# Loading the first four chunks of a gated linear attention two tokens to a partition, ahead of a fused MLP

## The chip, the cores and the metric

The kernel runs on one NeuronCore of a Trainium2 chip. The metric is device time in microseconds (us), taken over whole executions; five runs of the kernel before are shown, and one execution was recorded by the hardware profiler. Engines are named as in the profile: PE is TensorE's matmul side and PEld its weight loads, DVE is VectorE, ACT is ScalarE, POOL is GpSimd, SP is SyncE, which here only issues DMAs.

## The reference

Inputs q, k, v and alpha have the shape (4, 8, 768, 48): 4 batches, 8 heads, 768 tokens, 48 values a head, all f32. A recurrence with a decaying state gives the attention output, which then goes through an MLP with the gate h cos(h):

```
state = zeros(B, H, D, D)
for t in range(S):
    state = alpha[:, :, t, :, None] * state + k[:, :, t] (outer) v[:, :, t]
    y[:, :, t] = q[:, :, t] @ state
x = y as (B * S, H * D)            # 3072 tokens x 384
h = x @ w_in                       # 384 x 2048
out = (h * cos(h)) @ w_out         # 2048 x 384
```

## The kernel before

The recurrence is done in chunks of 128 tokens: 6 chunks a batch, 24 in all, and two neighbouring chunks make a pair (g = j // 2). Within a chunk, logarithms of alpha are summed by a matmul with a triangular matrix; exponentials of the sums scale k and q; scaled k and q are transposed; scores k·q are masked to the lower triangle; the output is scores times v plus the state of the chunk before times q; the state is updated and decayed. Heads are handled two at a time, in 64 rows each, of which 48 are used.

All work is written as units, a letter and a number each, and the string ORDER fixes the order in which they are issued. Each engine runs its own units in that order and each DMA queue too. The last loop of the kernel just walks through ORDER. The letters that matter here:

- `a k q v`: load of one chunk of alpha, k, q or v, on the SP queue (L158, L161): 128 partitions (tokens) by 8 heads by 48 values, so 1024 rows of 192 B, 192 KB.
- `w`: a half of w_in (w0, w1) or of w_out (w2, w3), on POOL's DMA queue, cast to bf16 on the way (L167, L171).
- `i`/`l`, `c`/`C`, `d`/`E`: logarithm on ACT (L185), cumulative sums on PE (L191, L193), two exponentials on ACT (L201, L202), for one chunk or for a pair.
- `K`/`B` and `R`/`O`: scaling of k (L206) and of q (L212), on POOL or on DVE. `P`: cast of v to bf16 on POOL (L216). `M`: the chunk's decay on POOL (L220).
- `T`, `t`: transposes on PE (L227) and their copy out of PSUM by DVE (L232). `D`: the same by a DMA transpose on the SP queue (L236).
- `A`, `m`: scores on PE (L243) and their masking on DVE (L248). `S`, `u`, `b`: the state's matmuls (L257), its update on DVE (L262 or L272), its decay on POOL (L262).
- `Y`, `y` or `Q`, `z`: outputs of a chunk or of a pair on PE (L298), copied to the MLP's input xT by DVE (L306, L317).
- `F`/`H`, `f`/`h`, `p`/`g`: first MLP product on PE (L337), cosine on ACT as a shifted sine (L343), gate on DVE (L348). F works on one chunk and half of the 2048 columns, H on a pair and a quarter. F0 and F2 need w0, F1 and F3 need w1. `V`: a quarter of the second product (L358); `e`: its copy by ACT (L362); `o`: store on the SP queue (L366).
- `x12`: twelve matmuls on zeros (L371), which keep PE running while it has nothing else.

ACT loads another function table whenever it passes from logarithms and exponentials to sines or back (L179, L343). PSUM is handed out from two small pools, 3 tiles of two banks (`two`) and 2 of one bank (`one`). An instruction that waits on one engine holds all that stand behind it on that engine, and a DMA that waits holds the rest of its queue. On the SP queue, each DMA from the ninth on also waits for the one eight places before it to have landed.

Of the kernel before, what the change touches and what calls it, by code (L numbers as in the profile page):

```python
# [9 lines left out]
FP = mybir.dt.float32  # L10
# [7 lines left out]
k1 a0 a3 a1 k0 v1 q0 a2 q2 i0 x12 c0 v3 d0 k2 M0 i1 x7 c1 k3 K0 d1 q1 K1 q3 P1 O0 x13 T0 v0 l1 t0  # L18
a5 x2 C1 E1 a4 v2 K2 q5 R2 K3 k5 x15 T2 O1 t2 T1 k4 A0 t1 q4 P0 x1 A1 w0 S1 S0 a6 u0 w1 u1 l2 M1
m0 R3 x8 C2 w2 m1 T3 E2 M2 Y0 w3 t3 A2 y0 P2 Y1 m2 b1 S2 A3 M3 P3 u2 M4 m3 b2 Q1 x6 F0 z1 y1 S3 f0  # L20
F2 p0 f2 x2 F3 p2 F1 f3 H6 p3 f1 H4 p1 h6 u3 V4 h4 g6 b3 V5 V0 g4 V1 v4 H5 a7 V2 h5 v5 R5 V3 g5 V6
a8 e0 K5 V7 a9 H7 K4 e1 q6 R4 T5 h7 V8 t5 k6 V9 g7 T4 v9 P4 V10 t4 v6 V11 l3 S4 e2 A4 q7 u4 A5 P5
C3 m4 b4 o2 V12 E3 m5 V13 k7 S5 Q2 l4 u5 M7 M6 o0 R6 C4 z2 a11 M5 K6 V14 E4 H10 v7 b5 q8 T6 P6 k8
H8 t6 h10 R7 q11 S6 a10 V15 h8 g10 K7 H9 q9 e3 u6 g8 M9 T7 k9 M8 h9 H11 t7 k10 P7 g9 V16 h11 v8 R8
S7 A6 u7 A7 o1 V17 m6 b7 V20 a13 m7 V21 V18 a12 l5 g11 Q3 o3 R9 C5 z3 v10 K8 V19 E5 H12 K9 D8 e4
R11 H14 D9 M10 P8 H13 h12 K10 o4 q10 k11 g12 S8 h13 V22 v11 V23 u8 h14 q12 g13 H15 b8 e5 P10 k12
g14 V28 M11 k13 h15 P9 S10 V29 a15 g15 V30 a14 A8 R10 l6 A9 m8 V31 v12 K11 C6 e7 m9 E6 S9 D10 P11
Q4 u9 b9 D11 V24 z4 R12 V25 u10 v13 H18 K12 v14 b10 H16 D12 h18 H19 q15 g18 h16 o5 P12 S11 g16 h19
H17 M12 v15 u11 o7 V26 g19 h17 V27 a16 P13 V32 g17 e6 M13 A10 q13 A11 m10 S12 V33 o6 l7 V34 a17
m11 C7 k14 Q5 E7 a18 u12 A12 z5 P15 V36 R15 V37 m12 K13 V38 H22 R13 M15 H20 D13 b11 h22 P14 H21  # L30
q19 g22 K14 h20 q17 q14 V35 g20 v16 h21 V39 k15 q21 e8 H23 g21 e9 o9 V40 h23 S13 V41 u13 R14 g23
A13 V44 b13 l8 D14 V45 m13 V46 K15 q20 V47 v17 C8 D15 Q6 E8 P16 q16 V42 z6 a19 e11 V43 M16 R17 k17
H24 o8 q18 P17 k16 M14 S14 a21 h24 H25 u14 b14 e10 g24 S15 h25 o10 H26 R16 k18 g25 V48 h26 K17 H27
u15 g26 D17 b15 V52 h27 V53 a20 K16 v18 A15 A14 a23 m15 V49 D16 l9 V50 m14 V54 v19 C9 g27 Q7 E9
K18 V55 z7 V51 R18 e13 H28 o13 e12 R19 a22 o12 S16 M18 D18 S17 u16 H30 h28 b16 o11 g28 H29 q23 P19
h30 k19 P18 v22 M17 u17 V60 q22 h29 g30 V56 H31 g29 l10 A17 A16 m17 V61 V62 K19 m16 h31 V57 D19
V58 g31 C10 k20 Q8 E10 V59 z8 V63 R20 e14 H32 o14 e15 b17 k21 o15 K20 S18 k23 S19 u18 H34 h32 v21
R21 u19 D20 M19 g32 H33 b19 h34 v20 K21 v23 V68 g34 h33 k22 M20 V64 D21 H35 g33 P21 l11 A18 A19
m18 V69 V70 P20 m19 M21 h35 V65 V66 g35 C11 Q9 E11 P22 V67 z9 P23 K23 V71 e16 H36 o16 e17 M22 R23
o17 S20 R22 D23 H38 u20 h36 b20 H37 g36 h38 K22 M23 S21 D22 g38 h37 V76 H39 u21 g37 b21 V72 h39  # L40
A21 A20 m21 V77 V78 m20 V73 V74 g39 A22 Q10 V75 z10 V79 e18 m22 H40 o18 e19 o19 S23 h40 S22 H42
u22 b22 g40 H41 h42 u23 V80 b23 g42 h41 H43 g41 A23 h43 V84 m23 V81 g43 V82 Q11 V83 z11 V85 e20
H45 o20 V86 h45 H44 g45 H47 h44 H46 g44 h47 V87 g47 h46 V88 e21 V89 g46 o21 V92 V93 V90 V91 V94
e22 V95 o22 e23 o23
# [22 lines left out]
def kernel(  # L67
# [21 lines left out]

    sb = ctx.enter_context(tc.tile_pool(name="sb", bufs=1))  # L90
# [20 lines left out]
    nc.vector.memset(halfpi, math.pi / 2.0)  # L111
    ident_bf = sb.tile([C, C], BF, tag="ident_bf")
# [11 lines left out]
    make_upper_triangular(nc, mask_f, 1.0, diag=True)  # L124
    m2 = sb.tile([C, 2], FP, tag="m2")
# [6 lines left out]
    a_t = ring("a_sb", [C, 2, H, D], FP, 4)  # L132
    k_t = ring("k_sb", [C, H, D], FP, 6)
    q_t = ring("q_sb", [C, H, D], FP, 6)
    v_t = ring("v_sb", [C, H, D], FP, 6)
# [20 lines left out]

    def load(bufs, src):
        return lambda j: nc.sync.dma_start(out=bufs[j % len(bufs)], in_=rows(src, j))  # L158

    def load_a(j):  # L160
        nc.sync.dma_start(out=a_t[j // 2 % 4][:, j % 2], in_=rows(alpha, j))  # L161
# [20 lines left out]
    def ln(j, n):  # L182
        lnset()
        g, s = j // 2, slice(j % 2, j % 2 + n)
        nc.scalar.activation(out=lnab[g % 2][:, s, :, 0:D], in_=a_t[g % 4][:, s], func=AF.Ln)  # L185

    def cums(j, n):
        t = two.take(("c", j)).rearrange("s (i x) -> s i x", i=2)
        for i in range(n):
            l = lnab[j // 2 % 2][:, (j + i) % 2]  # L190
            nc.tensor.matmul(t[:, i, 0:HD], triu_bf, l[:, :, 0:D], start=True, stop=True)  # L191
            for p in range(NP):
                nc.tensor.matmul(t[:, i, HD + p : HD + p + 1],  # L193
                                 l[:, 2 * p : 2 * p + 2].rearrange("s h d -> s (h d)"),
                                 ones_bf, start=True, stop=True)
# [9 lines left out]
    def scale_k(eng, j):  # L205
        eng.tensor_tensor(out=kqb[j % 4][:, 0, :, 0:D], in0=k_t[j % 6],  # L206
                                in1=icp_t[j // 2 % 3][:, j % 2].rearrange("s (h d) -> s h d", h=H),
                                op=ALU.mult)

    def scale_q(eng, j):  # L210
        cp = cp_t[j // 2 % 3][:, j % 2, 0:HD]
        eng.tensor_tensor(out=kqb[j % 4][:, 1, :, 0:D], in0=q_t[j % 6],  # L212
                          in1=cp.rearrange("s (h d) -> s h d", h=H), op=ALU.mult)

    def cast_v(j):
        nc.gpsimd.tensor_copy(out=vpb[j % 4][:, :, 0:D], in_=v_t[j % 6])  # L216
# [22 lines left out]
    def scores(j):  # L239
        t, kq = two.take(("A", j)), qkT[j % 4]  # L240
        for h in range(H):
            r, p = slice(64 * (h % 2), 64 * (h % 2) + D), h // 2
            nc.tensor.matmul(t[:, ACOL[h] * C : (ACOL[h] + 1) * C],  # L243
                             kq[r, p * C : (p + 1) * C],
                             kq[r, (NP + p) * C : (NP + p + 1) * C], start=True, stop=True)

    def mask_scores(j):
        nc.vector.tensor_tensor(  # L248
            out=A_t[j % 4].rearrange("s (h t) -> s h t", h=H),
            in0=two[("A", j)].rearrange("s (h t) -> s h t", h=H),  # L250
            in1=mask_f.unsqueeze(1).to_broadcast([C, H, C]), op=ALU.mult)
        two.give(("A", j))

    def state(j):
        t = one.take(("S", j))
        for p in range(NP):
            nc.tensor.matmul(t[:, p * 96 : (p + 1) * 96],  # L257
                             kqb[j % 4][:, 0, 2 * p : 2 * p + 2].rearrange("s h d -> s (h d)"),
                             vpb[j % 4][:, 2 * p : 2 * p + 2, 0:D], start=True, stop=True)
# [15 lines left out]

    def outputs(j, t):
        vs = vpb[j % 4].rearrange("s h e -> s (h e)")
        qT, A = qkT[j % 4], A_t[j % 4]
        U = ub[(j - 1) % 3].rearrange("r p e -> r (p e)")

        def group(g):
            p, r = g // 3, g % 3
            mms = []
            if j % NC != 0:
                mms.append((U[:, p * C + 32 * r : p * C + 32 * r + 32],
                            qT[:, (NP + p) * C : (NP + p + 1) * C]))
            for h, off in (((0, 0),), ((0, 32), (1, -16)), ((1, 16),))[r]:
                h += 2 * p
                mms.append((vs[:, h * VS + off : h * VS + off + 32],
                            A[:, ACOL[h] * C : (ACOL[h] + 1) * C]))  # L290
            return [(g // 4, i == 0, i == len(mms) - 1) + m for i, m in enumerate(mms)]

        streams = [sum((group(g) for g in range(c, 12, 4)), []) for c in range(4)]
        for i in range(max(map(len, streams))):
            for c, stream in enumerate(streams):
                if i < len(stream):
                    kt, start, stop, lhsT, rhs = stream[i]
                    nc.tensor.matmul(t[32 * c : 32 * c + 32, kt * C : (kt + 1) * C],  # L298
                                     lhsT, rhs, start=start, stop=stop, skip_group_check=True,
                                     tile_position=(0, 32 * c))  # L300
# [4 lines left out]
    def ev_outputs_one(j):  # L305
        nc.vector.tensor_copy(out=x_t[j // 2 % 3][:, :, j % 2],  # L306
                              in_=one[("y", j)][:, 0 : 3 * C].rearrange("r (k t) -> r k t", k=3))
        one.give(("y", j))
# [6 lines left out]
    def ev_outputs_two(g):  # L315
        t = two[("y", g)].rearrange("r (b x) -> r b x", b=2)[:, :, 0 : 3 * C]
        nc.vector.tensor_copy(out=x_t[g % 3].rearrange("r k b t -> r b k t"),  # L317
                              in_=t.rearrange("r b (k t) -> r b k t", k=3))
# [50 lines left out]
    def warmup(n):  # L369
# [3 lines left out]
        "a": load_a, "k": load(k_t, k), "q": load(q_t, q), "v": load(v_t, v), "w": load_w,  # L373
# [42 lines left out]
```

## Time and profile before

| what | value |
|---|---|
| median of 5 runs | 193.4 us (192.63 to 194.17) |
| the profiled execution: time, span | 193.4 us, 191.4 us |
| PE busy | 179.4 us, 94% |
| PEld busy | 128.1 us, 67% |
| DVE busy | 117.5 us, 61% |
| ACT busy | 119.9 us, 63% |
| POOL busy | 81.5 us, 43% |
| granted TensorE clock | 1.0 throughout |
| DMA moved | 31.26 MB in 123094 packets, 117184 of them under 512 B |

The page cuts the span into 40 slices of 4.8 us and gives the busy share of each engine and of DMA in tenths. The chain that ended last is followed back from the last instruction: at each step to what released it. A busy PE is not PE at its peak, since matmuls overlap; so below, PE's work is counted by the pitch of its units and not by busy time. DMA shares over 100% in a window come from packets that overlap on an engine.

### The profile page before, as it was taken

How to read it: one execution, taken by the hardware profiler on the slowest of the kernel's cores; microseconds unless marked ns; L12 is line 12 of the kernel's file. 1: busy time of each engine (PE TensorE's matmuls, PEld its weight loads, DVE VectorE, ACT ScalarE, POOL GpSimd, SP SyncE). 2: the span in 40 equal slices, each digit the busy share in tenths (PEclk: the TensorE clock that was granted, in tenths of full speed). 3: DMA queues.
4: the chain of work that ended last, by engine and by line, in shares of the span. 5: the costliest groups of instructions: out<-in, count | busy, mean ns of one | idle time of the engine just before them, and what ended most of it. 6: DMA issues, size and time to landing. Idle time of an engine off the chain costs nothing.

```text
span 191.4 us, 5137 instructions
## 1 busy us (share of the span) xinstructions
PE 179.4 (94%) x2170; PEld 128.1 (67%) x2170; DVE 117.5 (61%) x138; ACT 119.9 (63%) x133; POOL 81.5 (43%) x128
## 2 busy tenths in 40 slices
PE   7997879989999999997999998999989999999993
PEld 2444548957688587685786685686676776776861
DVE  5025784843857937929828528838648568696450
ACT  2540344744778678947749567799989992362632
POOL 3317950055285575562065455563055593030000
PEclk9999999999999999999999999999999999999999
DMA  6999999999989999999899999979979993200112
GB/s 123 189 187 189 145 191 189 185 202 178 196 191 188 194 228 180 183 194 193 181 212 176 200 166 225 219 152 220 196 127 234 201 169 72 86 3 0 45 41 82
DMA packets 123094, 31.26 MB, mean 163 GB/s; under 512 B 117184, under 2 KB 122304, under 8 KB 123072
## 3 DMA queue, kind: packets, MB, share of 16 engines
q1 hardware_dynamic: 120192, 27.80, 84.2%
q0 software_dynamic: 2880, 3.15, 10.3%
q8 instruction: 17, 0.28, 0.7%
q14 instruction: 5, 0.04, 0.1%
HBM read 25.17 MB, written 4.72 MB: 156 GB/s over the span
## 4 chain that ended last, share of the span: by engine, by line
PE 34%; DMA 22%; SPq 15%; issue 11%; POOL 10%; ACT 4%; DVE 2%; POOLq 0%; ACTq 0%; DVEq 0%
PE one L358 16%; PE two L337 12%; DMA w<-in_moe_w_out_dram 10%; SPq L158 9%; DMA v_sb<-in_v_dram 8%; POOL kqb L212 3%; DMA q_sb<-in_q_dram 3%; SPq L161 3%; POOL kqb L206 3%; SPq L236 2%; PE two L298 2%; ACT c_sb L343 2%; DVE g_sb L348 1%; SPq L366 1%; PE two L243 1%
## 5 line engine op out<-in xcount | busy, mean ns | idle before, releaser
L348 DVE TENSOR_TENSOR g_sb<-two,c_sb 128x1024 bf16<-128x1024 f32 x48 | 57.9, 1220 | 28.4 <-ACT c_sb L343 27.8
L358 PE MATMUL one<-w,g_sb 128*128 128x384 bf16 x384 | 69.6, 326 | 2.3 <-DVE g_sb L348 1.1
L337 PE MATMUL two<-xT,w 128*128 128x256 bf16 (+1 forms) x624 | 68.4, 264 | 1.0 <-DVE g_sb L348 1.0
L343 ACT ACTIVATE c_sb<-two,halfpi 128x1024 bf16<-128x1024 f32 x48 | 52.5, 1114 | 20.1 <-PE two L337 19.6
L337 PEld LDWEIGHTS <-w 128*128 128x128 bf16 x624 | 56.7, 98 | 9.6 <-issue 1.1
L358 PEld LDWEIGHTS <-g_sb 128*128 128x128 bf16 x384 | 35.5, 98 | 24.9 <-DVE g_sb L348 2.1
L206 POOL TENSOR_TENSOR kqb<-k_sb,icp 128x384 bf16<-128x384 f32 x24 | 23.9, 1001 | 20.7 <-DMA k_sb<-in_k_dram 14.0
L248 DVE TENSOR_TENSOR A_sb<-two,mask_f 128x1024 bf16<-128x1024 f32 x24 | 28.4, 1216 | 2.3 <-PE two L243 2.2
L262 POOL TENSOR_TENSOR ub<-sc,Em 128x384 bf16<-128x384 f32 x20 | 16.6, 832 | 28.1 <-DVE sc L272 26.8
L212 POOL TENSOR_TENSOR kqb<-q_sb,cp 128x384 bf16<-128x384 f32 x22 | 21.9, 1001 | 9.6 <-DMA q_sb<-in_q_dram 8.2
L216 POOL CAST vpb<-v_sb 128x384 bf16<-128x384 f32 x24 | 12.0, 506 | 21.7 <-DMA v_sb<-in_v_dram 19.8
L362 ACT ACTIVATE o_sb<-one 128x384 f32<-128x384 f32 x24 | 11.6, 493 | 14.9 <-PE one L358 14.4
L343 ACT ACT_TABLE_LOAD x11 | 14.1, 1283 | 9.2 <-PE two L337 5.8
L371 PE MATMUL one<-warm 128*128 128x512 bf16 x66 | 17.8, 417 | 1.9 <-DVE warm L102 1.2
L185 ACT ACTIVATE lnab<-a_sb 128x768 bf16<-128x768 f32 (+1 forms) x13 | 10.3, 794 | 12.4 <-DMA a_sb<-in_alpha_dram 12.3
L201 ACT ACTIVATE icp<-two 128x768 f32<-128x768 f32 (+1 forms) x13 | 9.9, 762 | 11.2 <-PE two L193 8.4
L272 DVE TENSOR_TENSOR sc<-one,ub 128x384 f32<-128x384 f32 x20 | 11.0, 551 | 9.0 <-PE one L257 6.2
L179 ACT ACT_TABLE_LOAD x11 | 14.1, 1283 | 0.9 <-PEq L400 0.7
L317 DVE CAST xT<-two 128x768 bf16<-128x768 f32 x11 | 10.5, 956 | 5.8 <-PE two L298 5.6
L371 PEld LDWEIGHTS <-warm 128*128 128x128 bf16 x66 | 6.5, 105 | 9.6 <-issue 3.6
L298 PE MATMUL two<-qkT,ub 128*32 128x128 bf16 x228 | 9.3, 221 | 0.9 <-POOL ub L262 0.9
L298 PE MATMUL two<-A_sb,vpb 128*32 128x128 bf16 x352 | 9.8, 220 | 0.2 <-DVE A_sb L248 0.2
(42 smaller groups left out, 108.3 us busy)
## 6 DMA issues: line engine op xcount, KB each, us to landing
k_sb<-in_k_dram SPq DMA_DIRECT2D x24, 192.0 KB, 4.6
a_sb<-in_alpha_dram SPq DMA_DIRECT2D x24, 192.0 KB, 4.2
v_sb<-in_v_dram SPq DMA_DIRECT2D x24, 192.0 KB, 4.4
q_sb<-in_q_dram SPq DMA_DIRECT2D x24, 192.0 KB, 4.4
out_dram<-o_sb SPq DMA_DIRECT2D x24, 192.0 KB, 3.0
w<-in_moe_w_in_dram POOLq DMA_DIRECT2D x2, 768.0 KB, 9.9
w<-in_moe_w_out_dram POOLq DMA_DIRECT2D x2, 768.0 KB, 17.6
qkT<-kqb SPq DMA_TRANSPOSE x16, 3.9
```

The lines of the kernel that those rows point to most:

```text
L158: return lambda j: nc.sync.dma_start(out=bufs[j % len(bufs)], in_=rows(src, j))
L179: nc.scalar.preload_act_table_set("natural_log_exp_and_others")
L206: eng.tensor_tensor(out=kqb[j % 4][:, 0, :, 0:D], in0=k_t[j % 6], in1=icp_t[j // 2 % 3][:, j % 2].rearrange("s (h d) -> s h d", h=H), op=A ...
L212: eng.tensor_tensor(out=kqb[j % 4][:, 1, :, 0:D], in0=q_t[j % 6], in1=cp.rearrange("s (h d) -> s h d", h=H), op=ALU.mult)
L248: nc.vector.tensor_tensor(out=A_t[j % 4].rearrange("s (h t) -> s h t", h=H), in0=two[("A", j)].rearrange("s (h t) -> s h t", h=H), in1=mas ...
L262: eng.tensor_tensor(out=ub[j % 3][:, :, 0:96].rearrange("r p (a e) -> r p a e", a=2), in0=src.rearrange("r p (a e) -> r p a e", a=2), in1= ...
L298: nc.tensor.matmul(t[32 * c : 32 * c + 32, kt * C : (kt + 1) * C], lhsT, rhs, start=start, stop=stop, skip_group_check=True, tile_position ...
L337: nc.tensor.matmul(t[:, m * n : (m + 1) * n], w1[:, kk, f * C : (f + 1) * C], x_t[g % 3][:, kk, bs].rearrange("r b t -> r (b t)"), start=( ...
L343: nc.scalar.activation(out=c_s.take((name, i)), in_=two[(name, i)], func=AF.Sin, bias=halfpi, scale=1.0)
L348: nc.vector.tensor_tensor(out=g_t[g % 3][:, fs, bs], in0=shaped(two[(name, i)], name), in1=shaped(c_s[(name, i)], name), op=ALU.mult)
L358: nc.tensor.matmul(one[("o", j)][:, 0:DM], g_t[j // 2 % 3][:, f, j % 2], w2[:, f], start=(f == 0), stop=(f == NF - 1))
L371: nc.tensor.matmul((one.free or two.free)[0][:, 0:512], warm[:, 0:C], warm, start=True, stop=True)
```

## The change

For the first two pairs (SG = 2, chunks 0 to 3) one DMA loads 256 tokens of a tensor with two consecutive tokens to a partition: still 1024 rows, of 384 B each. A partition p then holds tokens 2p and 2p + 1. So partitions 0 to 63 hold the first chunk of the pair and partitions 64 to 127 the second, and the two slots that held two chunks now hold the even and the odd tokens. The attention of these four chunks gets code of its own: the cumulative sums add an inclusive and a strict triangle, each cut at the middle; scores are made in blocks of 64 x 64, four times as many matmuls, and masked with a mask made of four blocks; state and outputs add up an even and an odd part, each on 64 partitions; the copies to xT put even and odd tokens back in turn. Rings of k, q and v become three tiles of a pair for six tiles of a chunk.

The order is written anew throughout. At the start, all eight pair loads are named ahead of most other work (`a0 k2 a2 k0 l0 q0 q2 v0 ... v2`); the two weight halves of w_in are apart (w1, then w0 behind P3, R3, b1 and P2 on POOL); F1 and F3 come before F2 and F0; 37 matmuls on zeros remain of 66; there is one DMA transpose more (17 for 16) and one pair of PE transposes less; four scalings of k and four more of q are on DVE instead of POOL; the last state update, S23, comes at the end.

The diff, cut to what is spoken of:

```diff
 ORDER = """
-k1 a0 a3 a1 k0 v1 q0 a2 q2 i0 x12 c0 v3 d0 k2 M0 i1 x7 c1 k3 K0 d1 q1 K1 q3 P1 O0 x13 T0 v0 l1 t0
-a5 x2 C1 E1 a4 v2 K2 q5 R2 K3 k5 x15 T2 O1 t2 T1 k4 A0 t1 q4 P0 x1 A1 w0 S1 S0 a6 u0 w1 u1 l2 M1
-m0 R3 x8 C2 w2 m1 T3 E2 M2 Y0 w3 t3 A2 y0 P2 Y1 m2 b1 S2 A3 M3 P3 u2 M4 m3 b2 Q1 x6 F0 z1 y1 S3 f0
-F2 p0 f2 x2 F3 p2 F1 f3 H6 p3 f1 H4 p1 h6 u3 V4 h4 g6 b3 V5 V0 g4 V1 v4 H5 a7 V2 h5 v5 R5 V3 g5 V6
...
+a0 k2 a2 k0 l0 q0 q2 v0 x10 C0 l1 E0 a4 a5 B1 O1 K0 R0 x5 C1 E1 q4 x6 T0 T1 t1 t0 K2 M0 P0 P1 x6
+A1 A0 S0 S1 m1 w1 l2 u0 u1 O2 m0 v2 K3 P3 M1 R3 x8 T2 C2 T3 t2 t3 Y0 Y1 A3 b1 M2 P2 w0 E2 y0 y1 S2
+S3 A2 k4 R4 u2 m3 m2 w2 M3 b2 K4 w3 q5 v5 k5 F1 F3 v4 a6 a7 f1 f3 Q1 p1 z1 p3 x2 T4 F2 F0 f2 f0 p2
+u3 p0 H5 H6 h6 t4 V4 H4 V0 V1 V5 g6 H7 V2 V3 b3 a8 a9 h4 h5 V6 V7 O5 g5 g4 q7 k9 k6 q6 k7 h7 P4 e0
...
     def load(bufs, src):
-        return lambda j: nc.sync.dma_start(out=bufs[j % len(bufs)], in_=rows(src, j))
+        def issue(j):
+            g = j // 2
+            if g < SG:
+                b, c = j // NC, j % NC
+                nc.sync.dma_start(
+                    out=bufs[g % len(bufs)].rearrange("s (h x) -> s h x", h=H),
+                    in_=src[b, :, c * C : (c + 2) * C, :].rearrange("h (p i) d -> p h (i d)", i=2))
+            else:
+                nc.sync.dma_start(out=slot(bufs, j), in_=rows(src, j))
+        return issue
...
     def scores(j):
         t, kq = two.take(("A", j)), qkT[j % 4]
+        if j // 2 < SG:
+            for p in range(NP):
+                for jj in range(2):
+                    qq = qkT[(j // 2 * 2 + jj) % 4]
+                    for h in (2 * p, 2 * p + 1):
+                        r = slice(64 * (h % 2), 64 * (h % 2) + 64)
+                        for c in range(2):
+                            o = ACOL[h] * C + HC * jj
+                            k0, q0 = p * C + HC * c, (NP + p) * C + HC * c
+                            nc.tensor.matmul(t[HC * c : HC * c + HC, o : o + HC],
+                                             kq[r, k0 : k0 + HC], qq[r, q0 : q0 + HC],
+                                             start=True, stop=True, skip_group_check=True)
+            return
...
+            for c in range(2):
+                r = slice(HC * c, HC * c + HC)
+                for i in range(2):
+                    for jj in range(2):
+                        src = strict_bf if (i, jj) == (1, 0) else mask_f
+                        nc.gpsimd.tensor_copy(out=mask2[r, i, jj], in_=src[r, r])
```

## The prediction

> **What bounds the kernel now.** I read the forty slices and the sum of the chain first, then the chain, then TensorE's timeline of the first 45 us, then the DMA view cut into windows. The profiled execution has a span of 191.4 us and a time of 193.4, which is also the median of the five runs: 2.0 us lie outside the span.
>
> ```profile
> PE   7997879989999999997999998999989999999993
> ...
> DMA  6999999999989999999899999979979993200112
> GB/s 123 189 187 189 145 191 189 185 202 178 196 191 188 194 228 180 183 194 193 181 212 176 200 166 225 219 152 220 196 127 234 201 169 72 86 3 0 45 41 82
> ...
> PE 34%; DMA 22%; SPq 15%; issue 11%; POOL 10%; ACT 4%; DVE 2%; POOLq 0%; ACTq 0%; DVEq 0%
> ```
>
> Two resources are full: DMA until about 157 us, TensorE (PE) from about 29 us to 188. The last 30 us have an empty DMA row and a full PE row. So the end is set by when the MLP matmuls begin, plus the PE work behind that point, plus stalls. The chain (start, duration) shows what the beginning hangs on: a load of v, its cast on POOL, the issue of the weights behind that cast, and 20 us of weights:
>
> ```profile
> 13.88 4.63 DMA v_sb<-in_v_dram
> ...
> 18.57 0.51 POOL vpb L216
> 19.07 1.65 POOL w L167 x2
> ...
> 22.96 19.82 DMA w<-in_moe_w_out_dram
> ...
> 42.82 2.76 PE one L358 x16
> ```
>
> PE's timeline:
>
> ```profile
> 28.01 1.47 PE L371 MATMUL one<-warm 128*128 128x512 bf16 x6
> 29.32 1.50 PE L337 MATMUL two<-xT,w 128*128 128x128 bf16 x24
> ...
> 42.82 2.76 PE L358 MATMUL one<-w,g_sb 128*128 128x384 bf16 x16 [0.85 <-DMA w<-in_moe_w_out_dram]
> ```
>
> The first MLP matmul is at 29.32; at 42.82 PE waits once, for the last piece of w_out. Up to 29 us PE does small attention pieces and 64 of the 66 warm matmuls. I priced each unit of ORDER by its pitch in the chain (F and H 1.31 us, V 0.65, C 0.52, T 0.45, A 0.28, S 0.17, Q 0.90, a warm matmul 0.22): behind the first F stand 150.4 us of PE work. 29.3 + 150.4 = 179.7, and PE ends at 188.1, so 8.4 us are stalls and pattern changes.
>
> The DMA view in three windows, 2 to 4, 4 to 19 and 22 to 30 us (packets, MB, busy share; overlapping packets go over 100%):
>
> ```profile
> q1 hardware_dynamic: 2217, 0.42, 109.6%
> ```
>
> ```profile
> q1 hardware_dynamic: 14917, 2.82, 139.0%
> ```
>
> ```profile
> q0 software_dynamic: 714, 1.43, 99.3%
> q1 hardware_dynamic: 468, 0.09, 10.0%
> ```
>
> Alone, the loads move 1110 and then 995 packets of 192 B a microsecond: a load of 1024 takes 0.92 us at best and 1.05 with its gaps. Beside weights (q0, 2048 B written per packet) the load queue falls to 468 packets in 8 us, none at first, then 90 a microsecond. A load caught by weights nearly stops.
>
> **What the change removes, adds and moves.** *Packets.* Sixteen loads (16 x 1.05 = 16.8 us of DMA) become eight pair loads of 1024 packets of 384 B. No packet of 384 B is in the trace. By its packet records the medians are 15 ns at 192 B and 65 ns at 1536 B (the stores); the line between gives 22.3 ns at 384 B, over 16 engines 1.43 us a pair. Ends: 1.05 (a packet costs what it did) and 2.1 (cost goes by bytes). [...] One more DMA transpose (17 for 16; 1024 packets of 18 ns by the median, 31 by the mean, so 1.2 to 2.0 us, taken as 1.6) leaves DMA 16.8 - 11.4 - 1.6 = 3.8 us less to do.
>
> *Start.* First packets flow at 1.95 us; data are usable about 1.15 us after a load's last packet (the eighth load ends at 10.0, its Ln starts at 11.22). Pairs come as a0 k2 a2 k0 q0 q2 v0, so a2 ends at 1.95 + 3 x 1.43 = 6.2 and v0 at 1.95 + 7 x 1.43 = 12.0. Then come a4 a5 q4 (3.15), and v2 at 16.6. ACT runs Ln(a0), Ln(a2), then the first exponential: 7.4 + 0.84 + 0.81 = 9.1. On POOL K0, R0 and K2 take 1.0 each and end by 12.3; P0 waits for v0 until 13.1; P0 and P1 (0.5 each) end at 14.1. There POOL issues w1, with no wait of its own. In before the first weight packet came 1.6 us after such an issue, so here at 15.7. v2, which needs until 16.6, still has 0.9 us to go, over 600 packets.
>
> *The wait that this adds.* The w1 half (384 packets at 90 a microsecond after 1.1 us of ramp, as from 20.65 on in before) holds DMA to 21.0. v2 finishes just behind, usable at 22.4. P3 waits for v2, and POOL is in order: behind P3 (0.5) stand M1 (0.2), R3 (1.0), b1 (0.84), M2 (0.2), P2 (0.5) and the issue of w0. R3 ends at 24.1; PE, also in order, has T3 (0.45) ahead of Y0 and Y1, then A3, S2, S3, A2 (3.2 us together with T3's eviction): F1 at 27.8 rather than 29.3. w0 issues at 25.7 and is usable after 1.6 + 5.4 + 1.1, at 33.8; F1, F3, Q1, two warm matmuls and T4 fill PE to 32 only, so F2 waits nearly 2 us. w2 and w3 follow in the same queue at 5.4 us each (1024 packets of 768 B at 190 a microsecond), so V2, the first user of w3, runs at 44.6; PE's own units from F2 at 33.8 (F0, H5, H6, V4, H4, V0, V1, V5, H7) get there at 44.4. PE has 135.8 us left at V2; before had 138.0 left at 42.82. 44.6 + 135.8 = 180.4 against 180.8: a gain of 0.4 us. The PE work behind the first F is 150.6 for 150.4, so the order itself removes none.
>
> *Middle.* Over the floor of 0.5 us per 10 us that the last stretch shows with DMA idle, PE's stalls from 45 to 150 us come to 5.5 us. With 3.8 us less for DMA to do and PE no earlier, loads run some 3 us further ahead; I take back 1.0 of the 5.5, since a load is not the only cause. ACT loads its table in 16 places for 22 (6 x 1.28 = 7.7 us), on an engine that is 63% busy: nothing, as it runs beside PE; without that cover, at most those 7.7.
>
> *Edits costed at nothing.* Matmuls of 64 rows or columns are not in the trace. Scores become 32 a chunk: at 16 ns each (56 of L298 in 0.90) 0.5 us, at the 43 ns of L257 1.4. Outputs become up to 56 a chunk, 0.9 to 2.4. Before F1 the wait for v2 covers most of them, Q1 is covered by the wait for w0; uncovered, 1 to 4 us for four chunks. Eight mask copies on POOL (0.1 to 0.2 each, L216 being 0.5 for six times the row) fall in its idle 5 us before the first Em. Eight scalings move from POOL (1.0) to DVE (0.7 to 1.3), which is 61% busy: between a gain and a loss of one microsecond. S23 with its state update comes last, 1.7 us beside the last store.
>
> Sum: 191.4 - 0.4 - 1.0 = 190.0 span, 192.0 us.
>
> **The rivals.** *v2 gets through.* If a pair takes 1.1 us or less, POOL's chain, ending 6 us after a2, and not v0 sets the issue of w1, and v2 is in before the weights. Then R3 ends near 17, F1 starts near 21.5, the four weight pieces follow without a gap, and V2 is near 38: 38 + 135.8 = 173.8, 7 us earlier. DMA has only 16.8 - 8.8 - 1.6 = 6.4 us less to do, so loads lead by no more than before, and I give 1.5 back: 188.0 us. For it: at 139% busy the 192 B packets waited for something besides their engine. Against: at 1.43 the margin misses by 0.9 us.
>
> *384 B packets cost by bytes: slower.* Place: the seven pairs that lead to v0, all on the start. At 2.1 us a pair everything from P0 to V2 is 7 x 0.67 = 4.7 us later: 191.4 - 0.4 + 4.7 = 195.7, less some 1.7 us of stalls that a late start spares, so 194.0 span, 196.0 us. It decides from 1.43 + 1.4 / 7 = 1.63 us a pair, where the gain of 0.4 + 1.0 is used up. [...]
>
> *The new order stalls in the middle.* a22, a23 and C11 are brought ahead of the last loads of chunks 16 to 21, 2.1 us of queue; PE waiting there in three or four places of before's longest kind (1.0 us) would make 194.5 us.
>
> That the loads do not get faster at all is the far end of the second.
>
> **How the numbers follow.** v2 stalled, as summed: 0.50 (192.0, its own range 190.0 to 194.0); v2 through 0.13 (188.0); cost by bytes 0.20 (196.0); stalls in the middle 0.17 (194.5). A difference of 0.5%, 1 us, is about what a measurement of this kernel can tell. Of the first case 0.32 is faster, 0.15 the same, 0.03 slower; the second is all faster; of the other two 0.04 is the same and 0.33 slower. So 0.45, 0.19 and 0.36. The range, 188.4 to 196.2, reaches to both outer cases and leaves out their far halves.
>
> **What would show it.** Right: the cast of v2 (the second pair's) waits for v_sb from about 17 to 22 us; the MLP's first matmul starts near 27.8, and soon one waits for w_in for about 2 us; 384 B packets have a median of 22 ns; q1 has some 113 thousand packets for 120. Wrong: that cast before 19 us and the MLP near 22 (first rival), pairs over 1.63 us (second), or PE gaps of 1 us between 100 and 150 us put down to a k, q or v load (third).

## The result, and the profile after

The changed kernel is faster: the ratio of its time to the time of the kernel before is 0.988, with a 95% interval of 0.985 to 0.990. Its median is 191.97 us over 23 executions (189.27 to 198.04), beside 193.26 for the kernel before over 44 (192.32 to 194.47); the ratio leaves out slow executions, which for the changed kernel are 8 of 24 with the profiled one (more than 1.5% above its fastest), so it is lower than the quotient of the two medians, 0.993. The profiled execution has a span of 189.3 us and a time of 191.12, so 1.8 us lie outside. The forecast of 192.0 is close, but the time got there by another road: the wait on which the forecast was built did not happen, and waits that no case of it named took what that set free.

The page of the changed kernel, first its slices and the shares of its chain. "issue" is time in which an engine waited for nothing that the profile can name:

```profile
PE   7967757999998999899998999999999999999992
PEclk9999979999999999999999999999999999999999
DMA  6999999978465899989989999999995864100032
...
q1 hardware_dynamic: 112928, 28.06, 72.2%
...
q8 instruction: 18, 0.29, 0.7%
...
PE 58%; issue 15%; DMA 8%; ACT 7%; DVE 7%; POOL 2%; SPq 1%; POOLq 0%; ACTq 0%; DVEq 0%
```

A slice is 4.7 us. DMA is nearly full until about 142 us, with a dip from 38 to 66 that the kernel before does not have, and PE is full from about 33. New is the 5 in PE's sixth slice (23.7 to 28.4 us), between sevens, with a 7 in the granted clock of the same slice. POOL's timeline shows what became of the wait for v2, the second pair's load of v (start, busy, instruction, and in brackets the idle time before it and who ended it):

```profile
12.07 0.96 POOL L269 CAST vpb<-v_sb 128x384 bf16<-128x384 f32 x2
12.97 0.93 POOL L207 DMA_DIRECT2D w<-in_moe_w_in_dram  x1
...
15.66 0.50 POOL L269 CAST vpb<-v_sb 128x384 bf16<-128x384 f32 x1 [0.74 <-DMA v_sb<-in_v_dram]
...
18.95 0.80 POOL L207 DMA_DIRECT2D w<-in_moe_w_in_dram  x1
```

The first half of the weights (w1) is issued at 12.97, and the cast of v2 at 15.66 waited 0.74 us, where the forecast had it wait from about 17 to 22 us. By the packet records v2's last packet ends at 15.3 and the first packet of the weights starts at 15.7: v2 gets through by 0.4 us. So POOL is free early and w0 is issued at 18.95, not at 25.7. PE's timeline shows where the time went then:

```profile
22.52 0.34 PE L303 MATMUL two<-qkT 64*64 64x64 bf16 x18
25.91 0.42 PE L303 MATMUL two<-qkT 64*64 64x64 bf16 x14 [3.05 <-issue]
26.27 4.27 PE L448 MATMUL two<-xT,w 128*128 128x128 bf16 x48
...
31.31 0.26 PE L388 MATMUL two<-qkT,ub 128*32 128x64 bf16 x10
32.66 0.29 PE L388 MATMUL two<-qkT,ub 128*32 128x64 bf16 x14 [1.08 <-issue]
...
34.33 5.46 PE L448 MATMUL two<-xT,w 128*128 128x128 bf16 x72
...
44.85 1.46 PE L469 MATMUL one<-w,g_sb 128*128 128x384 bf16 x8
```

In the middle of the 32 scores of chunk 2, between the 18th and the 19th, PE stands for 3.05 us. All operands of these scores are there, and no semaphore is waited for. Then the 48 matmuls of F1 and F3 take 4.27 us (a later experiment has them in 2.85), since the clock is down; a second stand of 1.08 us follows inside Q1. Windowed from 20 to 30 us (length, busy time and count of PE, PEld, DVE, ACT and POOL, then granted clock, DMA share and GB/s):

```profile
20.00:30.00 10.00, 6.73 (x198) 6.16 (x187) 4.44 (x6) 3.02 (x4) 4.75 (x6) 0.83 1.21 211
```

A mean clock of 0.83 over 10 us is 3.4 us at half speed, from 25.9 to 29.3; windowed alone, that stretch has a granted clock of 0.50.

**What the stand is.** Counted along PE's own stream, weight loads and matmuls together (2365 of each on the page), it lies behind 702 of them and the second behind 958: 256 apart. The expectations below count two instructions more and speak of 704 and 960, and so does this text. The page has a queue of its own for instructions, q8, with 18 packets of 16 KB here and 17 before, which is about one for every 256 of the 4730 and 4340 PE instructions (263 and 255). So 256 instructions are called a block here, the places between blocks boundaries, and the packet a block's fetch: a reading of these counts, as the trace does not say what a packet holds. The DMA view of 23 to 25 us has one of these packets among the weights:

```profile
q0 software_dynamic: 194, 0.40, 106.5%
q1 hardware_dynamic: 54, 0.01, 3.4%
q8 instruction: 1, 0.02, 3.0%
```

Put side by side: PE passes instruction 448 at 19.98; the next block's packet runs only from 23.54 to 24.50; PE goes on with instruction 704 at 25.91. From passing a boundary to having the block behind the next boundary takes 5.93 us here, and the 256 instructions between, now small matmuls of 64 columns, take PE only 2.9. At 704, passed at 25.91, it is the same again: packet from 30.18 to 31.07, PE on at 32.66. In the kernel before, the packet after 448 (passed at 26.1) ran from 29.82 to 30.78, just as late, but PE reached 704 only at 34.11, and nothing stood; the row of that stretch has no idle time in front of it:

```profile
32.60 5.46 PE L337 MATMUL two<-xT,w 128*128 128x128 bf16 x72
```

So the wait lies in the open in the changed kernel: PE stands 3.05 us while weights are loading, 0.40 MB of them in the two microseconds of the DMA view above.

### The profile page after: what moved, and what is told of

Read it like the earlier page. It is cut to its first block, busy times and chain, and to the rows that moved or that the text cites. A ratio compares the mean times of both kernels' runs of the same rounds, so it can differ in the third digit from the quotient of the medians.

```text
span 189.3 us, 5514 instructions
## 1 busy us (share of the span) xinstructions
PE 175.0 (92%) x2365; PEld 128.7 (68%) x2365; DVE 121.8 (64%) x153; ACT 110.6 (58%) x124; POOL 76.6 (40%) x130
## 3 DMA queue, kind: packets, MB, share of 16 engines
q1 hardware_dynamic: 112928, 28.06, 72.2%
## 4 chain that ended last, share of the span: by engine, by line
PE 58%; issue 15%; DMA 8%; ACT 7%; DVE 7%; POOL 2%; SPq 1%; POOLq 0%; ACTq 0%; DVEq 0%
PE one L469 22%; PE two L448 20%; PE two L388 4%; DVE g_sb L459 3%; DMA qkT<-kqb 3%; DMA a_sb<-in_alpha_dram 3%; ACT c_sb L454 3%; DMA out_dram<-o_sb 2%; PE two L309 2%; PE one L482 2%; PE two L244 2%; DVE A_sb L314 2%; PE one L334 2%; PE one L280 1%; ACT L454 1%
## 5 line engine op out<-in xcount | busy, mean ns | idle before, releaser
L448 PE MATMUL two<-xT,w 128*128 128x256 bf16 (+1 forms) x624 | 69.7, 269 | 2.3 <-DVE g_sb L459 2.3
L454 ACT ACTIVATE c_sb<-two,halfpi 128x1024 bf16<-128x1024 f32 x48 | 52.3, 1114 | 32.1 <-PE two L448 29.5
L259 POOL TENSOR_TENSOR kqb<-k_sb,icp 128x384 bf16<-128x384 f32 x20 | 20.4, 1018 | 13.0 <-PE one L334 5.1
L314 DVE TENSOR_TENSOR A_sb<-two,mask_f 128x1024 bf16<-128x1024 f32 x20 | 23.6, 1217 | 2.9 <-PE two L309 2.8
L265 POOL TENSOR_TENSOR kqb<-q_sb,cp 128x384 bf16<-128x384 f32 x18 | 18.4, 1020 | 15.7 <-issue 6.5
L254 ACT ACTIVATE icp<-two 128x768 f32<-128x768 f32 x12 | 9.7, 811 | 11.8 <-PE two L246 9.0
L225 ACT ACTIVATE lnab<-a_sb 128x768 bf16<-128x768 f32 x12 | 10.0, 841 | 7.1 <-DMA a_sb<-in_alpha_dram 7.0
L482 PE MATMUL one<-warm 128*128 128x512 bf16 x37 | 11.0, 445 | 2.9 <-DVE warm L106 1.2
L388 PE MATMUL two<-A_sb,vpb 128*32 128x128 bf16 (+1 forms) x384 | 10.0, 219 | 0.0
L388 PEld LDWEIGHTS <-vpb 128*32 128x32 bf16 (+1 forms) x448 | 9.1, 95 | 1.2 <-issue 1.0
L388 PE MATMUL two<-qkT,ub 128*32 128x128 bf16 (+1 forms) x252 | 8.8, 216 | 1.1 <-issue 1.1
## 6 DMA issues: line engine op xcount, KB each, us to landing
out_dram<-o_sb SPq DMA_DIRECT2D x24, 192.0 KB, 3.0
a_sb<-in_alpha_dram SPq DMA_DIRECT2D x20, 192.0 KB, 3.7
q_sb<-in_q_dram SPq DMA_DIRECT2D x20, 192.0 KB, 3.8
k_sb<-in_k_dram SPq DMA_DIRECT2D x20, 192.0 KB, 4.0
v_sb<-in_v_dram SPq DMA_DIRECT2D x20, 192.0 KB, 3.9
```

Of the source, the lines that this page charges most:

```text
L259: eng.tensor_tensor(out=kqb[j % 4][:, 0, :, 0:D], in0=slot(k_t, j), in1=icp_t[j // 2 % 3][:, j % 2].rearrange("s (h d) -> s h d", h=H), op ...
L265: eng.tensor_tensor(out=kqb[j % 4][:, 1, :, 0:D], in0=slot(q_t, j), in1=cp.rearrange("s (h d) -> s h d", h=H), op=ALU.mult)
L314: nc.vector.tensor_tensor(out=A_t[j % 4].rearrange("s (h t) -> s h t", h=H), in0=two[("A", j)].rearrange("s (h t) -> s h t", h=H), in1=(ma ...
L388: nc.tensor.matmul(t[32 * c : 32 * c + 32, c0 : c0 + n], lhsT, rhs, start=start, stop=stop, skip_group_check=True)
L448: nc.tensor.matmul(t[:, m * n : (m + 1) * n], w1[:, kk, f * C : (f + 1) * C], x_t[g % 3][:, kk, bs].rearrange("r b t -> r (b t)"), start=( ...
L454: nc.scalar.activation(out=c_s.take((name, i)), in_=two[(name, i)], func=AF.Sin, bias=halfpi, scale=1.0)
```

## The experiments

The theory: the loads by pairs let v2 pass ahead of the weights, as the first rival had it, and some 5.5 us of that rival's gain (stands of 3.05 and 1.08, and 4.27 - 2.85 = 1.42 of slow clock) went into instruction blocks that came late. The rivals to it: the stand belongs to the 64 x 64 scores themselves, or it is a wait for data that the trace does not name; and for the gain, that it comes from the new order or the new code rather than the packets.

**Fewer instructions, same work.** The score matmuls of this code take the query columns of both chunks at once, and so do the outputs: 100 matmuls and their 100 weight loads less, ORDER unchanged.

```diff
-    qkT = ring("qkT", [C, 2 * NP * C], BF, 4)
+    qk_all = sb.tile([C, 4, 2 * NP * C], BF, tag="qkT", name="qkT")
+    qkT = [qk_all[:, i] for i in range(4)]
...
-                            nc.tensor.matmul(t[HC * c : HC * c + HC, o : o + HC],
-                                             kq[r, k0 : k0 + HC], qq[r, q0 : q0 + HC],
+                        nc.tensor.matmul(t[HC * c : HC * c + HC, o : o + C],
+                                         kq[r, k0 : k0 + HC], qk_all[r, b0 : b0 + 2, q0 : q0 + HC],
...
-            return [(HC * i, HC, lhsT, qkT[(j // 2 * 2 + i) % 4][:, c0 : c0 + HC]) for i in range(2)]
+            return [(0, C, lhsT, qk_all[:, b0 : b0 + 2, c0 : c0 + HC])]
```

> The changed kernel, with qkT as one tile, so that one matmul takes the 64 columns of both chunks of a pair: 64 score matmuls and 36 output matmuls fewer, each with its weight load, 200 PE instructions in all; the same products. Theory (PE instructions come in blocks of 256; while weights load a block takes some 6 us from when the block before last is left, and PE stood 3.05 us in the scores of chunk 2 for one): the stall leaves the scores of chunk 2, first MLP matmul near 23 us instead of 26.3, no slice with a lower clock, a shorter stall at a later boundary (up to 2.5 us); span 185 to 187.5 us, ratio to the kernel before 0.965 to 0.980. Rival (PE waits there for something else, such as a copy by DVE or a load): stall stays, first MLP matmul at 26 us, span 189, ratio 0.988.

Measured: ratio 0.974 (0.969 to 0.979), span 186.9. PE's timeline of this kernel:

```profile
22.52 0.42 PE L303 MATMUL two<-qkT 64*64 64x128 bf16 x16
22.87 2.85 PE L449 MATMUL two<-xT,w 128*128 128x128 bf16 x48
...
25.94 0.23 PE L389 MATMUL two<-A_sb,vpb 64*32 64x128 bf16 x2
27.50 0.62 PE L389 MATMUL two<-A_sb,vpb 64*32 64x128 bf16 x30 [1.34 <-issue]
```

The scores of chunk 2 begin at 22.52 in both kernels, so the smaller count saved PE no time before them; 32 small scores took 0.45 us and 16 larger ones 0.42. But nothing stands in them any more: the MLP begins at 22.87 and its first 48 matmuls take 2.85 us at full clock. The stand is 1.34 us and lies in Q1, in quite other matmuls, again exactly at instruction 704. This settles that the place is a count and not an operation. One point was missed: a slice with a lower clock was to be gone, and it came later, from 28.6 to 32.0 us, behind the shorter stand:

```profile
PEclk9999996999999999999999999999999999999998
```

The kernel also beats both others: against the changed kernel the intervals do not overlap.

**w0 behind R4 on POOL, with the same instructions**, so that fewer weights are in flight when the block is fetched.

```diff
-... A3 b1 M2 P2 w0 E2 y0 y1 S2 S3 A2 k4 R4 u2 ...
+... A3 b1 M2 P2 E2 y0 y1 S2 S3 A2 k4 R4 w0 u2 ...
```

> The changed kernel, with the issue of w0 moved on POOL from behind P2 to behind R4, nothing else. Theory (the block of PE instructions that PE asks for near 20 us is held up by w0's packets, which begin at 22.0): w0's packets begin near 24, the block is in before them, no stall in the scores of chunk 2, first MLP matmul near 23 us at full clock; F2 then waits for w0 until about 29.5, a block stall of 1 to 2 us may come in Q1; span 186 to 188. Rival (code size alone, whatever DMA carries): the stall of 3 us stays where it is and w0 is merely later: span 189.5 to 191.

Measured: 0.982 (0.978 to 0.987), not to be told from the changed kernel's 0.988 (0.985 to 0.990). Its PE timeline:

```profile
24.82 0.31 PE L303 MATMUL two<-qkT 64*64 64x64 bf16 x14 [1.95 <-issue]
25.07 4.47 PE L448 MATMUL two<-xT,w 128*128 128x128 bf16 x48
```

The stand stays at 704 but shrinks from 3.05 to 1.95 us, as the packet starts at 22.36 instead of 23.54. The expectation, no stand and an MLP at full clock near 23 us, was missed. By the packet records w1's own packets still run until 21.2 here, 1.2 us past the boundary; then no weights move until w0's first packet at 23.5. So w0 was not alone in front of the fetch.

**The same rows as before, in the new code and the new order.** Each pair load becomes two DMAs with rows of 192 B.

```diff
-                nc.sync.dma_start(
-                    out=bufs[g % len(bufs)].rearrange("s (h x) -> s h x", h=H),
-                    in_=src[b, :, c * C : (c + 2) * C, :].rearrange("h (p i) d -> p h (i d)", i=2))
+                t = src[b, :, c * C : (c + 2) * C, :].rearrange("h (p i) d -> p i h d", i=2)
+                for i in range(2):
+                    nc.sync.dma_start(out=both(bufs, g)[:, i], in_=t[:, i])
```

> The changed kernel with its layout, code and order, but each pair load cut into two DMAs, one for even and one for odd tokens, so packets of 192 B again (16 loads for 8). Theory (the gain at the start is the packet size, 1.21 us a pair against 2 x 1.03): the cast of v0 moves by 5 to 6 us, to 17.5; first MLP matmul at 31 to 34, depending on whether the second pair's v is caught by w1; span 193.5 to 196.5, ratio 1.01 to 1.025. Rival (the order and the fewer warm matmuls make the gain): span within 1 us of 189.3.

Measured: 1.023 (1.019 to 1.027), span 197.4: the ratio within what was expected, the span above it. POOL's timeline:

```profile
16.67 0.93 POOL L207 DMA_DIRECT2D w<-in_moe_w_in_dram  x1
...
26.38 0.50 POOL L269 CAST vpb<-v_sb 128x384 bf16<-128x384 f32 x1 [7.76 <-DMA v_sb<-in_v_dram]
...
29.33 0.80 POOL L207 DMA_DIRECT2D w<-in_moe_w_in_dram  x1
```

This is the wait of the forecast's main case, complete: v2 is caught by w1, its cast stands 7.76 us, w0 comes at 29.33 and the MLP's first matmul at 33.86. Rows of 192 B, with the sixteen DMAs that they take, cost 0.035 of the time, 6.8 us, and decide on which side of the weights v2 falls. Part of that is the clock, which is at half from 25.0 to 38.7 us.

**The loads and the code of before in the new order** (the switch SG at 0; the first four chunks by two loads of 192 B rows where a pair load stood).

```diff
-    SG = 2
+    SG = 0
...
+            for jj in (j, j + 1) if j < 4 else (j,):
+                nc.sync.dma_start(out=slot(bufs, jj), in_=rows(src, jj))
```

> The new order with the old code for chunks 0 to 3: one token to a partition, two loads of 192 B rows in place of each pair load, old matmuls (SG = 0). Theory: loads as late as with cut pair loads, but 465 PE instructions fewer, so no stall for a block of instructions: first MLP matmul at 28 to 30, 3 to 4 us ahead of the cut pair loads; span 190 to 192, ratio 0.993 to 1.003. Rival (own code costs nothing): within 1 us of the run with cut pair loads.

A miss: 1.042 (1.037 to 1.046), span 198.5, where the 465 PE instructions less were to make it faster than the run before. The waits of PE in this kernel (total, times, longest):

```profile
PE one L274 <- POOL kqb L259: 6.3, 1, 6.3
PE two L303 <- DMA qkT<-kqb: 4.8, 3, 2.5
```

The first is the caught v2 again, seen from PE through POOL's queue. The second are stands in the second half, at 120.6, 141.2 and 165.3 us, for DMA transposes that come late. So the new order with the loads and the code of before loses. With the same rows and the pairs' attention code it ran at 1.023, without these stands (0.2 us in all for DMA transposes), so nothing here shows that code to cost time. Why the DMA transposes come late in this kernel and not in that one is open.

**w1 ahead of K2 on POOL**, 2 us earlier, with the fast loads kept.

```diff
-... T0 T1 t1 t0 K2 M0 P0 P1 x6 A1 A0 S0 S1 m1 w1 l2 ...
+... T0 T1 t1 t0 w1 K2 M0 P0 P1 x6 A1 A0 S0 S1 m1 l2 ...
```

> The changed kernel, with the issue of w1 moved on POOL ahead of K2, M0, P0 and P1 (some 2 us earlier), nothing else. Theory (the second pair's v escaped w1 in the changed kernel only by its margin: last packet near 15.0 us, first weight packet 15.7): w1's packets now begin near 13.7, v is caught, its cast on POOL moves from 15.7 to 19.5 to 21 us and the first MLP matmul would come 3 us later, but the stall at PE's instruction 704 is then covered by it: first MLP matmul at 25.5 to 27.5, span 187.5 to 191. Rival (weights do not stop a load of 384 B packets as they stop 192 B ones): cast at 16 to 17 us and everything as in the changed kernel.

Measured: 0.998 (0.995 to 1.002), span 191.9, F1 at 27.82; both a little beyond what was expected. POOL's timeline:

```profile
10.87 0.93 POOL L207 DMA_DIRECT2D w<-in_moe_w_in_dram  x1
...
20.62 0.50 POOL L269 CAST vpb<-v_sb 128x384 bf16<-128x384 f32 x1 [5.79 <-DMA v_sb<-in_v_dram]
```

Issued 2.1 us sooner, the weights catch v2 at 384 B too, and the whole gain is gone. F1 at 27.82 is just what the forecast's main case had, but by another sum: the cast of v2 is at 20.6, not at 22.4, and the clock is at half from 21.9 to 32.1 us, from within a wait of 2.90 us that PE has behind v2. The stand at 704 has vanished, as PE now takes 4.0 us from one boundary to the next: the two delays hide each other.

**Both together:** the merged matmuls and w0 behind R4.

> Both earlier edits at once: merged matmuls (200 PE instructions fewer) and w0 issued behind R4. Theory (blocks of 256 PE instructions, fetched late beside weights): PE reaches instruction 704 in Q1 near 26 us, and the block asked for near 21 us is in by 25: no stall there; first MLP matmul near 23 us at full clock; F2 waits for w0 until 29.5; instruction 960 near 32, with a stall under 1 us. Span 184.5 to 186.5, ratio 0.958 to 0.972, 1 to 2 us less than with merged matmuls alone. Rival (w0's own lateness costs as much as the stall it removes): span 186.5 to 188.

Measured: 0.981 (0.977 to 0.985), span 187.1, against 186.9 with the merged matmuls alone. PE's timeline:

```profile
22.65 2.85 PE L449 MATMUL two<-xT,w 128*128 128x128 bf16 x48
...
25.71 0.63 PE L389 MATMUL two<-A_sb,vpb 64*32 64x128 bf16 x32
...
30.14 2.10 PE L449 MATMUL two<-xT,w 128*128 128x128 bf16 x18 [1.98 <-DMA w<-in_moe_w_in_dram]
```

Instruction 704, within the row at 25.71, is now passed without a stand, but F2 then waits 1.98 us for the later w0. That is what the rival named: the next bound stands close behind. For the fetch this pair of runs says more than the time does. With the merged matmuls alone, w1's packets end and w0's begin within 0.2 us of the boundary 448 (20.95), and the block's packet starts 4.1 us after it. Here w0 begins only at 23.2, and the packet starts 1.3 us after the boundary.

**The merged matmuls, with Q1 behind F2 and F0**, to have large matmuls at the boundary.

```diff
-... F1 F3 v4 a6 a7 f1 f3 Q1 p1 z1 p3 x2 T4 F2 F0 f2 f0 p2
+... F1 F3 v4 a6 a7 f1 f3 p1 p3 x2 T4 F2 F0 Q1 f2 f0 z1 p2
```

> Merged matmuls as before, with Q1 and its eviction moved behind F2 and F0 in ORDER, w0 in its old place. Theory: instruction 704 then lies in F2, which waits for w0 until about 27.5 anyway, so that stall costs nothing; the next one, instruction 960, comes behind Q1 instead of inside F0 and is in near 34 us as before: 1 to 1.5 us less than with merged matmuls alone, span 185 to 187. Rival (H5 and its gates come later, and the pipeline of ACT and DVE behind them loses it): span 187 to 189.

Measured: 0.992 (0.989 to 0.995), span 190.3, worse than the merged matmuls alone and than either expectation. PE's timeline:

```profile
29.90 2.85 PE L449 MATMUL two<-xT,w 128*128 128x128 bf16 x48 [3.00 <-DMA w<-in_moe_w_in_dram]
...
35.64 2.72 PE L449 MATMUL two<-xT,w 128*128 128x256 bf16 x12 [1.15 <-DVE xT L425]
```

Without Q1 as filling, F2 waits 3.00 us for w0, and the next product waits for the outputs of Q1. The rival was right in its direction. The expectation had w0 usable near 27.5; its last packet ends at 29.6 here, and PE goes on 0.3 us later. In the changed kernel w0 was issued 0.7 us sooner and its last packet ends at 27.3, so there F2 could have begun near 27.7 (an estimate from that 0.3). 34.33 - 5.5 = 28.8 is later than that: in the changed kernel all of the 5.5 us held F2 back. Why w0 took longer here is open.

**The kernel before, with its instruction count moved.** Its warm matmuls ahead of the first F are cut finer, 116 of 64 columns for 14 of 512, so that 204 PE instructions are added and boundary 704 falls just ahead of the MLP.

```diff
-m0 R3 x8 C2 w2 ... m3 b2 Q1 x6 F0 z1 y1 S3 f0
+m0 R3 X64 C2 w2 ... m3 b2 Q1 X52 F0 z1 y1 S3 f0
```

> The kernel before, with 14 of its matmuls on zeros (8 and 6 of 512 columns, 3.0 us) replaced by 116 of 64 columns (3.1 us): the same work and nearly the same PE time, but 204 PE instructions more ahead of the first MLP matmul. Theory (code length itself costs, while weights load): PE crosses instruction 448 near 22.5 us and reaches 704 near 27.5, a block stall of 1 to 2 us appears there, exactly at instruction 704, where the kernel before has none; span 192 to 193.5, ratio 1.003 to 1.011. Rival (the stall belongs to the new code's 64-row matmuls or to the new order): no stall, span 191.4 within 0.5, ratio 0.998 to 1.003.

PE's timeline:

```profile
28.30 1.08 PE L375 MATMUL one<-warm 128*128 128x64 bf16 x31
30.18 0.79 PE L375 MATMUL one<-warm 128*128 128x64 bf16 x21 [0.80 <-issue]
```

A stand of 0.80 us put down to nothing appears in the kernel before as well, at instruction 704, between two matmuls on the same zeros. For the place this is as clean as it can be, though the stand was to be 1 to 2 us. For the time it says nothing: the ratio is 1.002 (0.9996 to 1.005), and the matmuls that stood had no work to do.

## Why the prediction came out right, and where it did not

*Packets.* The median of a 384 B packet is 22 ns, as taken from the line between 192 and 1536 B, and q1 has 112928 packets for the forecast 113 thousand. The step that failed is the next: dividing by 16 engines to get 1.43 us a pair. The loads end 1.21 us apart (4.88, 6.09, 7.30, 8.53), and in the DMA view of 4 to 10 us:

```profile
q1 hardware_dynamic: 5137, 1.94, 116.6%
```

5137 packets in 6 us are 856 a microsecond, 1.20 us a pair, with packets overlapping on their engines to 116.6%. The windows of before had shown that overlap, 109.6% and 139.0%, and the forecast had quoted it as a mark for the rival without using it. The upper end of the main case's own range, 194.0, is 2.0 us over its sum; over the seven pairs that lead to v0 that would be pairs of 1.72 us (an estimate), which no run shows: they were 1.21 apart. How much dearer a packet of 384 B is depends on the rate that is taken for 192 B: 1.20 over 0.92 is 1.30, over 1.05 it is 1.14. But in the changed kernel, just behind the pair loads, rows of 192 B move faster (11 to 12 us) than at the start of the kernel before, which comes near that only much later (1345 from 76.5 to 77.5 us):

```profile
q1 hardware_dynamic: 1360, 0.26, 127.5%
```

That is 0.75 us a load of 1024, and 1.20 over 0.75 is 1.59. So the two sizes were not compared at one rate in the forecast, and what held the first loads of before to 995 to 1110 is not shown.

*Who wins, v2 or the weights.* The first rival had its mechanism right, and its point (1.1 us a pair or less) too narrow. The first weight packet came at 15.7, just as forecast, but by two errors that cancel: w1 was issued at 12.97 and not at 14.1, and from there the packet took 2.7 us, not the 1.6 of before. So one term decided, the arrival of v2: its last packet ended at 15.3, for 16.6. POOL's chain did set w1's issue: P0 had no wait for v0, and K0 and R0 were 1.31 us where 1.0 was taken. That the forecast's main case is a real mechanism at this place is shown twice, with 192 B rows and with w1 earlier. It had the wrong side of a margin of 0.4 us.

*Start.* With v2 through, F1 should have been at 21.5 by the rival and at 27.8 by the main case; it was at 26.3. Without the stand it is at 22.87, so the rival was 1.4 us early, and the stand made up the rest. F2, that the main case had at 33.8 after a wait for w0, came at 34.33 without a wait for w0, after the stands and the slow clock. V2 came at 44.85 for 44.6. Two errors of the opposite sign and nearly the same size met here: v2 did not cost 27.8 - 22.87 = 4.9 us, and the instruction blocks cost some 5.5. The rival's 188.0 is nearly what the merged kernel ran at (188.66 in its profiled execution, median 189.07), but not by the rival's sum: V2 is at 42.3 there and not near 38, and less is lost behind it.

*Middle.* With 135.8 us of PE work left at V2, the last MLP matmul ends at 185.7. That makes the start worth 0.15 us (180.65 for 180.8; forecast 0.4), and what is lost behind V2 went from 7.3 to 5.05 us: 2.25, for the 1.0 "taken back". The tail gave 0.3 back. Together 2.1 us of span, for 1.4. So nearly all of the measured gain lies behind V2, and the forecast's reason for it, that loads run further ahead, is not borne out. With rows of 192 B in the same order and code V2 is at 52.17 and the last MLP matmul ends at 193.50, so 5.53 us are lost, nearly as little as here. PE's recorded waits behind 45 us add up to 2.9 us before and 2.8 after, and none of them is for a load. So what changed is no wait that the trace names, and the run speaks for the new order and code, not for the loads; which part of them is open. It is no clean test, since its MLP began 7.6 us later.

*The other rivals.* Cost by bytes is refuted by 1.20 us a pair, the point being 1.63. Stalls in the middle from the new order did not come: from 45 us on PE has three gaps over 0.5 us, of 0.56, 1.01 and 0.70, all put down to the gate on DVE and none to a load; before has 1.00, 0.84 and 0.62. The order did stall in the middle with the old loads and code, by DMA transposes, but not with rows of 192 B in the new code.

*Edits costed at nothing.* Matmuls of 64 x 64 run at 14 ns each (32 in 0.45 us), below the lower bound of 16. What the forecast left out is that each of them is an instruction with a weight load beside it, and that the 390 PE instructions which the change adds in all shift where the blocks of 256 begin and shorten the time that a block lasts (2.9 us from 448 to 704, not counting the stand, for 8.0 before).

What stays open: whether the weight transfers hold the fetch up, and by what. At the boundary 448 the block's packet started 1.3 to 1.8 us after it in the three runs where no weight packet ran over the next 1.5 us but for the first 0.2 (both together, rows of 192 B, w1 early), 2.4 us where w1's end was in the way, and 2.9 to 4.1 us in those where weights ran on. Loads moved meanwhile at up to 1282 packets a microsecond in one of the three, which points to the weights and not to DMA work as such. The nearest to a test are the two runs with merged matmuls, which differ in the issue of w0 alone, with one profiled execution each. The executions of the changed kernel spread over 8.8 us and those of the kernel before over 2.2. A fetch that comes now sooner and now later may be behind it, or a v2 that is caught in some executions: in the run with Q1 later, its last packet ended 0.2 us behind the first of the weights. No run tested either.

## What to carry to other kernels

When a load must pass ahead of a bulk transfer, work out both arrival times to within a microsecond, with the throughput of packets (1.20 us a pair here) and not their durations over 16 engines (1.43): the margin was 0.4 us here, and issuing the weights 2.1 us sooner took the whole gain. A gap of an engine that the trace puts down to nothing ("issue") is to be looked up in the instruction queue: count the instructions to it, and if it moves with the count and not with the work, use fewer and larger instructions there (100 matmuls fewer, with their weight loads, cut a stand of 3.05 us to 1.34 here). A gain is to be tied to the edit that is said to make it: here most of it lay behind the place that the short loads serve, and was there with the old rows too. A delay taken away early can lay bare another one right behind it, so a forecast that agrees with the time is to be checked at its steps.

## What the runs showed of the hardware

- PE stood at counts of its instructions that lie 256 apart, 704 and 960 in the changed kernel, and the instruction queue had a packet of 16 KB for about every 256 of them (18 for 4730, 17 for 4340). From passing a boundary to going on behind the next took 4.3 to 6.8 us around the weight transfers, where PE had to wait; PE stood for 0.25 to 3.05 us. In the changed kernel it went on 1.4 and 1.6 us after the packet that followed the boundary before had ended (24.50 to 25.91, 31.07 to 32.66). The packets themselves took 0.88 to 1.55 us in the two kernels.
- The granted clock fell to half after short stands among small matmuls: 3.4 us of it after stands of 3.05, 1.95 and 1.34 us (the changed kernel, with 0.50 from 25.9 to 29.3; w0 behind R4, a mean of 0.83 from 20 to 30; merged matmuls, 0.72 from 27 to 33). It stayed at 1.00 after the stand of 1.08 us in the changed kernel and after the one of 0.80 us in the kernel before with its count moved.
- Loads with rows of 384 B moved 856 packets a microsecond. Those with rows of 192 B moved 995 to 1110 at the start of the kernel before, 1345 at one place later in it, and up to 1360 in the changed one: doubling the row cost 14 to 59% a packet, by the rate that is taken.
- A load caught by weights came late: the cast of v2 stood 5.79 us with rows of 384 B and 7.76 with 192.
- Where POOL and DVE scaled at once, at least one of them was slower: POOL took 1.31 us instead of 1.00 in the changed kernel; in the kernel before POOL kept to 1.00 and the scaling on DVE took 1.26 instead of 0.68.
